# A chunkwise mLSTM cell with a gated MLP: the first chunk's attention in halves of 64 tokens, two batches at a time, and keys and queries loaded ahead of all else

## The chip, the cores and the metric

The kernel runs on one core of a Trainium2 chip. The time is that of one execution on the device in microseconds (us), as a median of several runs. A core has TensorE (PE: matmuls; PEld: its weight loads), VectorE (DVE), ScalarE (ACT), GpSimd (POOL) and SyncE (SP, which issues all the DMAs here). Each engine works through its own instructions in order and waits for the others by semaphores.

## What is computed

The first part is an mLSTM cell, a recurrence over tokens with a matrix state for each of 4x8 heads of width 40:

```python
# B, H, S, D = 4, 8, 768, 40
for t in range(S):
    m_new = np.maximum(f_gate[:, :, t] + m, i_gate[:, :, t])
    f_stab = np.exp(f_gate[:, :, t] + m - m_new)
    i_stab = np.exp(i_gate[:, :, t] - m_new)
    m = m_new
    C = f_stab[:, :, None, None] * C + i_stab[:, :, None, None] * np.einsum('bhd,bhe->bhde', vt, kt)
    n = f_stab[:, :, None] * n + i_stab[:, :, None] * kt
    h_tilde = np.einsum('bhde,bhe->bhd', C, qt)
    denom = np.maximum(np.abs(np.einsum('bhd,bhd->bh', n, qt)[:, :, None]), 1.0)
    y[:, :, t] = 1.0 / (1.0 + np.exp(-o_gate[:, :, t])) * h_tilde / denom
```

Its output, as 3072 tokens of 320 columns, goes through an MLP: `h = x @ w_in` (320 to 2048 columns), `g = h * sigmoid(1.702 h)`, `g @ w_out` (back to 320). The weights come as 64-bit floats, which the kernel turns into 32-bit ones itself.

## The kernel before

The 768 tokens are cut into 6 chunks of L = 128, for all 4 batches at once (512 tokens of the MLP per chunk). Chunk w needs: its gates' running sums (`gates`), the decay factors as columns (`columns`), keys and queries with head width on partitions (`transposes`), weights between tokens (exponentials of gate differences times scores), the sum over values (`values`), the carried state, and the normalised and gated result (`outputs`) transposed for the MLP (`seam`). Then the up-projection runs over 8 pairs of 128 hidden columns (`up` for chunk 0, `up_fast` for the others), then the down-projection in blocks. The attention of chunk w+1 is put between the down blocks of chunk w by a list written out by hand (`attention`).

Chunks from 1 on work in halves of HL = 64 tokens and on two batches at a time (index c): the scores are then 64x64 blocks on the diagonal, the state is carried to the middle of the chunk (`state_mid`) and to its end, and each half gets its share from the state before it. There `slot(i, x)` says in which half of the 128 partitions the half x of the heads of parity i lies; parities 0 and 1 lie crossed, so that the blocks use all four corners of the TensorE array.

Chunk 0 is different before the change. It has no state before it, and its attention is done on whole blocks of 128x128 tokens, one batch b at a time. `weights(0, b)` adds up the exponents on TensorE in PSUM: a mask (L366), then for each head the running maximum `m3` (L370) and the gate sums `a3` (L371), both split in three 16-bit parts, and ACT takes Exp (L373). `scores(0, b)` multiplies queries and keys (L390), and DVE multiplies the two (L392). `values(0, b)` is one matmul per head (L432). One `carry` per two batches gives the state at the chunk's end (L493), copied by ACT (L497), between the up-projections of chunk 0; `scale` (L483, on POOL) weights the values for it.

The order of the start is that of the program text: the loads are issued on SP by `load` (L121, keys, queries, values, gates of one batch) and `fetch` (L166, a piece of the MLP weights); the pieces are turned into 32-bit floats by `convert`, two operations on ACT (L234, L235) and four on DVE (L236 to L241). `up(0, 0)` needs pieces 0 to 2. `keep_busy(n)` puts n matmuls without use on TensorE (L189). The loop at L718 interleaves transposes, scores, weights and two converts; the loop at L731 does values, outputs and seams; L765 starts `up`, whose first matmul is L515. PSUM tiles come from two pools: `banks` gives pairs of banks from `ps_a` (two such tiles), other tiles come from `ps_m` (four, one of which belongs to the idle matmuls).

Of the kernel before, what the change touches and what calls it, by code (L numbers as in the profile page):

```python
# [26 lines left out]
def kernel(  # L27
# [140 lines left out]
    wt = {(0, b): gp.tile([L, NP, 2, L], FP, tag="g", name="wt") for b in range(B)}  # L168
    load_gates(0)
    for b in range(B):  # L170
        load(0, "kq", slice(b, b + 1))
        if b:
            fetch(b - 1)
    for b in range(B):
        load(0, "vo", slice(b, b + 1))
    for n in range(3, 10):
        fetch(n)
# [3 lines left out]
    idle, ident_b, neg_mask = (small[:, n * 128:n * 128 + 128] for n in range(3))  # L181
    pick = small[0:3 * BH, 384:384 + BH]
    a3, m3 = (small[0:3 * BH, n * 128:n * 128 + 128] for n in (4, 5))
    V.memset(idle, 0.0)
    p_idle = ps_m.tile([128, W], FP, tag="m", name="p_idle")

    def keep_busy(n):
        for _ in range(n):
# [13 lines left out]
    G.affine_select(out=neg_mask, in_=neg_mask, compare_op=OP.is_ge, fill=NEG, base=0, pattern=[[1, L]],  # L202
                    channel_multiplier=-1)
# [15 lines left out]
    for t in (k_0, q_st):  # L219
        G.memset(t[:, :, D:DP], 0.0)  # L220
# [23 lines left out]
    def gates(w):  # L244
# [37 lines left out]
        for x, (old, new) in enumerate(((m, mid), (mid, end)) if w else ((m, end),)):  # L282
            t = slice(x * HL, x * HL + HL) if w else slice(0, L)
            V.tensor_scalar(out=st[BH:2 * BH, t], in0=m_run[:, t], scalar1=old, scalar2=None, op0=OP.subtract)
            V.tensor_scalar(out=st[2 * BH:3 * BH, t], in0=a[:, t], scalar1=new, scalar2=-1.0, op0=OP.subtract,
                            op1=OP.mult)
# [4 lines left out]
        if w:  # L291
            dec[w] = gate.tile([BH, 2, BH // 2], FP, name="dec")
            both = gate.tile([BH, 2], FP, name="both")
            V.tensor_tensor(out=both[:, 0:1], in0=m, in1=mid, op=OP.subtract)
            V.tensor_tensor(out=both[:, 1:2], in0=mid, in1=end, op=OP.subtract)
            for x in range(2):
                V.tensor_scalar(out=dec[w][:, x, :], in0=pair, scalar1=both[:, x:x + 1], scalar2=None, op0=OP.mult)

    def slot(i, x):

        return slice((x ^ i) * HL, (x ^ i) * HL + HL)
# [10 lines left out]
    def columns(w):  # L312
        pt = banks("p_cols")[:, 0, :]
        st = stacked[w]
        if w:
            T.matmul(pt[:, 0:3 * BH], st[0], keep, start=True, stop=False)
            T.matmul(pt[:, 0:3 * BH], st[1], swap, start=False, stop=True)
        else:
            T.transpose(pt[:, 0:3 * BH], st, full)
        n = 3 * BH  # L320
        if w in dec:
            n += BH
            T.matmul(pt[:, 3 * BH:n], half.rearrange("p a b -> p (a b)"), dec[w].rearrange("p a b -> p (a b)"),
                     start=True, stop=True)
        c = cols[w] = gate.tile([L, 4 * BH], FP, name="cols")
        V.tensor_copy(out=c[:, 0:BH], in_=pt[:, 0:BH])
        A.activation(out=c[:, BH:3 * BH], in_=pt[:, BH:3 * BH], func=AF.Exp, scale=-1.0)
        if w in dec:
            A.activation(out=c[:, 3 * BH:n], in_=pt[:, 3 * BH:n], func=AF.Exp)
# [4 lines left out]
    def transposes(w, b):  # L334
        for dst, name in ((kT, "kT"), (qT, "qT")):
            dst[w, b] = work.tile([128, NP, L], FP, tag=name, bufs=4, name=name)
        pt = banks("p_t")
        for x, src in enumerate((k_of(w), q_st)):
            for p in range(NP):
                h = b * H + 2 * p  # L340
                T.transpose(pt[:, x, p * L:(p + 1) * L], src[:, h:h + 2, :].rearrange("p a b -> p (a b)"), ident)  # L341
        for x, (dst, copy) in enumerate(((kT, A.copy), (qT, V.tensor_copy if w else A.copy))):
            copy(out=dst[w, b].rearrange("r j t -> r (j t)"), in_=pt[:, x, :])
# [8 lines left out]
    def spread(w):  # L352

        for c in range(2):
            x = wt[w, c] = work.tile([L, NJ, 2, HL], FP, tag="wt", bufs=2, name="wt")
            for i in range(2):
                for n in range(2):
                    src = m_row[w][c * PH + i:(c + 1) * PH:2, n * HL:(n + 1) * HL]
                    nc.sync.dma_start(out=x[slot(i, n), :, i, :], in_=src.unsqueeze(0).to_broadcast([HL, NJ, HL]))

    def weights(w, c):
        if w == 0:
            x = wt[w, c]
            pw = banks("p_w").rearrange("s i (p t) -> s i p t", t=L)
            for i in range(2):
                T.matmul(pw[:, i], ident_b, neg_mask.unsqueeze(1).to_broadcast([L, NP, L]), start=True, stop=False)  # L366
                for p in range(NP):
                    h = c * H + 2 * p + i
                    one = pick[:, h:h + 1].to_broadcast([3 * BH, L])
                    T.matmul(pw[:, i, p, :], one, m3, start=False, stop=False)  # L370
                    T.matmul(pw[:, i, p, :], a3, one, start=False, stop=(p == NP - 1))  # L371
            for i in range(2):
                A.activation(out=x[:, :, i, :], in_=pw[:, i], func=AF.Exp)  # L373
            return
# [9 lines left out]
    def scores(w, c):  # L384
        if w == 0:
            pw = [ps_m.tile([L, NP, L], FP, tag="m", name="p_s") for _ in range(2)]
            for p in range(NP):
                for i in range(2):
                    r = slice(i * 64, i * 64 + D)
                    T.matmul(pw[i][:, p, :], kT[w, c][r, p, :], qT[w, c][r, p, :], start=True, stop=True)  # L390
            for i in range(2):
                V.tensor_tensor(out=wt[w, c][:, :, i, :], in0=pw[i], in1=wt[w, c][:, :, i, :], op=OP.mult)  # L392
            return
        pw = banks("p_s")
        for j in range(NJ):
            b, p = 2 * c + j // NP, j % NP
            for i in range(2):
                r = slice(i * 64, i * 64 + D)
                for x in range(2):
                    t = slice(x * HL, x * HL + HL)  # L400
                    T.matmul(pw[slot(i, x), i, j * HL:(j + 1) * HL], kT[w, b][r, p, slot(i, x) if w == 1 else t],  # L401
                             qT[w, b][r, p, t], start=True, stop=True)
# [22 lines left out]
    def values(w, c):  # L425
        if w == 0:
            hs = slice(c * H, (c + 1) * H)
            po = ps_m.tile([L, H, D1], FP, tag="m", name="p_o")
            for p in range(NP):
                for i in range(2):  # L430
                    h = 2 * p + i
                    T.matmul(po[:, h, :], wt[w, c][:, p, i, :], v_st[:, c * H + h, :], start=True, stop=True)  # L432
            outputs(w, hs, po)
            return
# [3 lines left out]
        for j in range(NJ):  # L438
            for i in range(2):
                for x in range(2):  # L440
                    t, r = slice(x * HL, x * HL + HL), slot(i, x)
# [43 lines left out]
    def carry(w, c):  # L485
        js = slice(c * NJ, (c + 1) * NJ)
        pc = banks("p_c")
        n = 2 if 0 < w < NW - 1 else 1
        for j in range(NJ):
            for i in range(2):  # L490
                for x in range(n):
                    t = slot(i, x) if w else slice(0, L)
                    T.matmul(pc[i * 64:i * 64 + 64, x, j * D1:(j + 1) * D1], k_cols(w, t, c * PH + 2 * j + i),  # L493
                             vw[w, c][t, 2 * j + i, :], start=True, stop=True)
        new = lambda x: pc[:, x, 0:NJ * D1].rearrange("r (j d) -> r j d", d=D1)
        if w == 0:
            A.copy(out=state[1][:, js], in_=new(0))  # L497
            return
        for x, dst in enumerate((state_mid, state[1 - w % 2])[:n]):
            if x:  # L500
                decay(w, c, x, V)
            V.tensor_tensor(out=dst[:, js], in0=new(x), in1=dst[:, js], op=OP.add)
# [209 lines left out]
    gates(0)  # L712
    G.memset(k_1[:, :, D:DP], 0.0)
# [3 lines left out]
    G.memset(v_st[:, :, D:D1], 1.0)  # L717
    for b in range(B + 1):  # L718
        if b < B:
            transposes(0, b)  # L720
        if b:
            scores(0, b - 1)
        if b < B:
            weights(0, b)
        if 0 < b < 3:
            convert(b - 1)
    load(1, "kq")
    load_gates(1)
    columns(0)
    keep_busy(4)  # L730
    for b in range(B + 1):  # L731
        if b < B:
            hs = slice(b * H, (b + 1) * H)
            A.activation(out=eo[0][:, hs, :], in_=eo[0][:, hs, :], func=AF.Tanh, scale=0.5)
            values(0, b)
            if b == 1:
                convert(2)
            keep_busy(2)
        if b == B:
            keep_busy(3)  # L740
        if b:
            seam(0, (b - 1) // 2, ((b - 1) % 2,))
# [12 lines left out]
    def attention(w):  # L755
        at = (0, 1, 3, 4, 8, 9, 10, 11, 13) if w == 1 else (0, 1, 2, 4, 6, 7, 8, 9, 11)
        calls = [[(columns, w), (decay, w, 0, 0), (decay, w, 1, 0), (scale, w, 0), (scale, w, 1)],
                 [(weights, w, 0)], [(weights, w, 1), (open_gates, w)], [(carry, w, 0), (carry, w, 1)],
# [3 lines left out]
    for w in range(NW):  # L762
        more = w + 1 < NW
        if w == 0:
            for j in range(NF // 2):  # L765
# [5 lines left out]
                if j < B:  # L771
                    (carry if j % 2 else scale)(0, j // 2)
# [77 lines left out]
```

## Time and profile before

| what | value |
|---|---|
| median of 3 runs (486.65 to 486.68) | 486.67 us |
| the profiled execution | 486.67 us |
| its span, from first to last instruction | 485.0 us |
| first matmul of the first up-projection (L515) | 34.09 us |
| TensorE busy, 0 to 34.09 | 31.50 us, idle matmuls included |
| DVE, ACT, POOL busy, 0 to 34.09 | 22.98, 16.57, 9.77 us |
| DMA engines busy, 0 to 34.09 | 0.97 of the time, 209 GB/s |
| TensorE busy, 34.09 to 76.14 | 42.05 us of 42.05 |

The profile lists instructions with their engine, the line in the code, the tiles (out<-in) and shapes. A matmul in 32-bit floats appears as two records. The chain of work that ended last is followed back from the last instruction: at each step to what released it, or to the instruction before it on its engine. Times in a timeline are from the start of the span.

### The profile page before, as it was taken

To read this page: it belongs to the slowest core of one execution; us is meant where nothing else is said; L and a number is where in the kernel's file an instruction comes from. 1 tells how busy PE (TensorE), PEld (TensorE's weight loads), DVE (VectorE), ACT (ScalarE), POOL (GpSimd) and SP (SyncE) were. 2 spreads that over 40 slices of the span, in tenths; PEclk is the share of its full clock that TensorE was granted. 3 is DMA by queue.
4 is the path that set the end of the run, shared out by engine and by line. 5 is a ranking of instruction groups with operands and counts; after the bars stand their busy time and mean duration, and the time that the engine had idled before them with its cause. 6 is when DMAs were issued, how large, how long until landed. Compare 5 with 4: busy or idle time off the path is not lost.

```text
span 485.0 us, 12103 instructions
## 1 busy us (share of the span) xinstructions
PE 479.3 (99%) x5016; PEld 388.0 (80%) x5016; DVE 344.0 (71%) x680; ACT 195.3 (40%) x434; POOL 149.7 (31%) x145
## 2 busy tenths in 40 slices
PE   8999999999999999999999999999999999999997
PEld 5774447777767999767999877999876999876997
DVE  6675976988778966768967668968677958343812
ACT  3746557801453901444811354720264630164200
POOL 6020003400398610127620136630035640035300
PEclk9999999999999999999999999999999999999999
DMA  8999995005992000999000899000799000000000
GB/s 176 182 285 146 254 206 153 2 18 103 208 157 45 3 30 3 174 185 139 1 31 3 153 189 158 1 31 3 127 195 165 10 30 3 29 0 1 0 28 27
DMA packets 130790, 44.31 MB, mean 91 GB/s; under 512 B 105616, under 2 KB 128176, under 8 KB 130736
## 3 DMA queue, kind: packets, MB, share of 16 engines
q1 hardware_dynamic: 130736, 43.55, 50.3%
q8 instruction: 39, 0.64, 0.6%
q14 instruction: 15, 0.12, 0.1%
HBM read 39.52 MB, written 4.01 MB: 90 GB/s over the span
## 4 chain that ended last, share of the span: by engine, by line
PE 95%; DVE 3%; POOL 1%; ACT 0%; issue 0%; POOLq 0%; DVEq 0%
PE p_out L687 32%; PE p_h L585 26%; PE p_h L590 8%; PE p_out L636 7%; PE p_h L515 6%; PE p_c L493 3%; PE p_o L442 2%; PE p_s L401 2%; PE p_i L450 2%; PE p_h L521 2%; PE p_x L466 1%; PE p_t L341 1%; PE p_o L432 1%; PE p_s L390 0%; DVE wt L392 0%
## 5 line engine op out<-in xcount | busy, mean ns | idle before, releaser
L627 POOL TENSOR_TENSOR g<-g,parts 128x512 f32<-128x512 f32 x30 | 38.3, 1276 | 124.4 <-DVE parts L619 113.3
L687 PE MATMUL p_out<-w_out_sb,g 128*128 128x160 f32 x480 | 71.0, 302 | 0.0
L687 PEld LDWEIGHTS p_out<-w_out_sb,g 128*128 128x128 f32 x480 | 66.6, 190 | 0.9
L585 PE MATMUL p_h<-xT,w_in_sb 128*128 128x256 f32 x240 | 66.9, 388 | 0.0
L566 ACT ACTIVATE g<-g 128x512 f32<-128x512 f32 x80 | 50.0, 631 | 35.3 <-DVE g L622 24.8
L585 PEld LDWEIGHTS p_h<-xT,w_in_sb 128*128 128x128 f32 x240 | 43.8, 190 | 20.2 <-issue 7.6
L468 ACT COPY xT<-p_x 128x768 f32<-128x768 f32 (+1 forms) x14 | 9.9, 707 | 114.1 <-PE p_x L466 114.1
L692 DVE TENSOR_TENSOR o_sb<-o_sb,p_out 128x160 f32<-128x160 f32 x70 | 21.0, 316 | 44.2 <-PE p_out L687 43.8
L687 PE MATMUL p_out<-t_sb,s 128*128 128x160 f32 x320 | 47.1, 300 | 0.0
L687 PEld LDWEIGHTS p_out<-t_sb,s 128*128 128x128 f32 x320 | 44.4, 190 | 0.2
L618 DVE TENSOR_TENSOR t_x<-p_h,parts 128x256 f32<-128x256 f32 x40 | 16.8, 419 | 38.9 <-PE p_h L590 34.3
L585 PE MATMUL p_h<-t_x,s_in 128*128 128x256 f32 x160 | 41.1, 379 | 0.0
L590 PE MATMUL p_h<-xT,w_in_x 64*128 64x512 f32 x160 | 39.7, 615 | 0.0
L377 ACT ACTIVATE wt<-wt,cols 128x64 f32<-128x64 f32 x160 | 38.8, 338 | 0.0
L423 POOL COPY y<-y 128x128 f32<-128x128 f32 (+1 forms) x14 | 4.0, 285 | 108.7 <-DVE y L420 108.7
L636 PE MATMUL p_out<-w_out_sb,g 128*128 128x320 f32 x128 | 36.3, 437 | 0.0
L585 PEld LDWEIGHTS p_h<-t_x,s_in 128*128 128x128 f32 x160 | 30.4, 190 | 4.1
L615 ACT COPY parts<-p_h 128x256 f32<-128x256 f32 x40 | 14.9, 374 | 45.9 <-PE p_h L585 45.9
L636 PEld LDWEIGHTS p_out<-w_out_sb,g 128*128 128x128 f32 x128 | 23.6, 190 | 9.2 <-DVE w_out_sb L241 0.2
L619 DVE TENSOR_TENSOR parts<-p_h,t_x 128x512 f32<-128x512 f32 x40 | 27.7, 692 | 4.2
L626 ACT COPY g<-p_h 128x512 f32<-128x512 f32 x30 | 17.4, 580 | 30.5 <-PE p_h L590 25.2
L515 PE MATMUL p_h<-xT,w_in_sb 128*128 128x512 f32 x64 | 29.5, 604 | 0.1
(192 smaller groups left out, 897.5 us busy)
## 6 DMA issues: line engine op xcount, KB each, us to landing
wt<-m_row SPq DMA_DIRECT2D x40, 128.0 KB, 4.3
k_sq<-in_k_dram SPq DMA_DIRECT2D x16, 320.0 KB, 5.9
q_sq<-in_q_dram SPq DMA_DIRECT2D x16, 320.0 KB, 10.1
out_dram<-o_sb SPq DMA_DIRECT2D x24, 160.0 KB, 1.8
eo<-in_o_gate_dram SPq DMA_DIRECT2D x5, 640.0 KB, 10.0
bits<-in_moe_w_in_dram SPq DMA_DIRECT2D x6, 512.0 KB, 9.0
v_st<-in_v_dram SPq DMA_DIRECT2D x14, 160.0 KB, 5.2
bits<-in_moe_w_out_dram SPq DMA_DIRECT2D x6, 320.0 KB, 4.8
```

Of the source, the lines that this page charges most:

```text
L377: A.activation(out=x[:, h, :], in_=x[:, h, :], func=AF.Exp, scale=-1.0, bias=cols[w][:, c * PH + h:c * PH + h + 1])
L515: T.matmul(ph[j][i], w_in_sb[:, c, f * 128:(f + 1) * 128], x[:, c, :], start=(first and c == 0), stop=(not first and c == 1))
L566: A.activation(out=gs[w, j][:, i, :], in_=gs[w, j][:, i, :], func=AF.Gelu_apprx_sigmoid)
L585: T.matmul(out, a, x[n], start=start, stop=stop)
L590: T.matmul(row, w_in_x[r, j, :], rest_x[r, 2, :], start=not late, stop=late)
L618: V.tensor_tensor(out=u2, in0=both[:, 1, right], in1=y[:, left], op=OP.add)
L619: V.tensor_tensor(out=y[:, half_w:3 * half_w].rearrange("p (a t) -> p a t", a=2), in0=flat[:, half_w:3 * half_w].rearrange("p (a t) -> p a ...
L626: A.copy(out=g[:, 0, :], in_=row0)
L627: G.tensor_tensor(out=g0, in0=g0, in1=u, op=OP.add)
L636: T.matmul(po, gs[w, f // 2][:, f % 2, b * L:(b + 1) * L], w_out_sb[:, f, :], start=(f == 0), stop=(f == NF - 1))
L687: T.matmul(po, a(f), b[:, f, :], start=(f == 0), stop=(f == NH - 1))
L692: V.tensor_tensor(out=dst, in0=x, in1=po, op=OP.add)
```

## The change

Chunk 0 takes the halves too. `slot` gets the chunk: in chunk 0 half x lies in half x of the partitions, for both parities. `weights`, `scores` and `values` lose their branch for chunk 0; a new function `exponents` adds its exponents on TensorE for two batches, by halves. Chunk 0 now has a `dec` and a middle state, `columns(0)` makes the decay columns for it, `carry` takes the list of halves to do, the first state is set to zero, and the two halves of the carry stand apart: the one to the middle before `values`, the one to the end between the up-projections. Keys and queries of all batches are loaded first; values and output gates are loaded for two batches at a time, between the first two weight pieces. Two pad fills go from POOL to DVE. The order of the start is written anew.

```diff
-    wt = {(0, b): gp.tile([L, NP, 2, L], FP, tag="g", name="wt") for b in range(B)}
+    wt = {}
     load_gates(0)
     for b in range(B):
         load(0, "kq", slice(b, b + 1))
-        if b:
-            fetch(b - 1)
-    for b in range(B):
-        load(0, "vo", slice(b, b + 1))
-    for n in range(3, 10):
+    load(0, "v", slice(0, 2))
+    fetch(0)
+    load(0, "v", slice(2, 4))
+    load(0, "o", slice(0, 2))
+    fetch(1)
+    load(0, "o", slice(2, 4))
+    for n in range(2, 10):
         fetch(n)
...
     V.memset(idle, 0.0)
+    for t in (k_0, q_st):
+        V.memset(t[:, :, D:DP], 0.0)
...
-    for t in (k_0, q_st):
-        G.memset(t[:, :, D:DP], 0.0)
...
-        for x, (old, new) in enumerate(((m, mid), (mid, end)) if w else ((m, end),)):
-            t = slice(x * HL, x * HL + HL) if w else slice(0, L)
+        for x, (old, new) in enumerate(((m, mid), (mid, end))):
+            t = slice(x * HL, x * HL + HL)
...
-    def slot(i, x):
-
-        return slice((x ^ i) * HL, (x ^ i) * HL + HL)
+    def slot(w, i, x):
+
+        n = x ^ i if w else x
+        return slice(n * HL, n * HL + HL)
...
+    def exponents(c):
+
+        x = wt[0, c] = work.tile([L, NJ, 2, HL], FP, tag="wt", bufs=2, name="wt")
+        pw = banks("p_w")
+        for i in range(2):
+            for r in (slice(0, HL), slice(HL, L)):
+                T.matmul(pw[r, i, :], ident_b[:, r], neg_mask.unsqueeze(1).to_broadcast([L, NJ, HL]), start=True,
+                         stop=False)
+            hs = pick[:, c * PH + i:(c + 1) * PH:2].unsqueeze(2).to_broadcast([3 * BH, NJ, HL])
+            for r in (slice(0, HL), slice(HL, L)):
+                T.matmul(pw[r, i, :], a3[:, r], hs, start=False, stop=False)
+            for j in range(NJ):
+                h = c * PH + 2 * j + i
+                for r in (slice(0, HL), slice(HL, L)):
+                    T.matmul(pw[r, i, j * HL:(j + 1) * HL], pick[:, h:h + 1].to_broadcast([3 * BH, HL]), m3[:, r],
+                             start=False, stop=(j == NJ - 1))
+        A.activation(out=x.rearrange("s j i t -> s i j t"), in_=pw.rearrange("s i (j t) -> s i j t", t=HL), func=AF.Exp)
...
-    def carry(w, c):
+    def carry(w, c, xs):
...
+        for x in xs:
+            new, dst = pc[:, x, 0:NJ * D1].rearrange("r (j d) -> r j d", d=D1), (state_mid, state[1 - w % 2])[x]
+            if w == x == 0:
+                A.copy(out=dst[:, js], in_=new)
+                continue
             if x:
                 decay(w, c, x, V)
-            V.tensor_tensor(out=dst[:, js], in0=new(x), in1=dst[:, js], op=OP.add)
+            V.tensor_tensor(out=dst[:, js], in0=new, in1=dst[:, js], op=OP.add)
...
     gates(0)
+    G.memset(v_st[:, :, D:D1], 1.0)
+    G.memset(state[0], 0.0)
...
+    transposes(0, 0)
+    transposes(0, 1)
+    exponents(0)
+    scores(0, 0)
+    transposes(0, 2)
+    exponents(1)
+    convert(0)
+    transposes(0, 3)
+    columns(0)
+    scores(0, 1)
+    for c in range(2):
+        scale(0, c)
+    for c in range(2):
+        carry(0, c, (0,))
     load(1, "kq")
     load_gates(1)
...
+    convert(1)
+    for c in range(2):
+        hs = slice(c * PH, (c + 1) * PH)
+        A.activation(out=eo[0][:, hs, :], in_=eo[0][:, hs, :], func=AF.Tanh, scale=0.5)
+        keep_busy(3)
+        values(0, c)
+    convert(2)
+    keep_busy(6)
+    seam(0, 0)
+    keep_busy(6)
+    seam(0, 1)
     keep_busy(2)
...
-                    (carry if j % 2 else scale)(0, j // 2)
+                    run([(carry, 0, j // 2, (1,)) if j % 2 else (scale, 0, j // 2)])
```

In the changed program the first matmul of the first up-projection is at L504, the values at L433, the state's share at L441, the outputs' first two passes at L447 and L448, the carries at L482, the scores at L401, the scaling at L474.

## The prediction

> **What bounds the kernel now.** I read the page first, then the chain of work that ended last, then the timeline of the first 36 us, and the DMA issues there one at a time.
>
> ```profile
> span 485.0 us, 12103 instructions
> PE 479.3 (99%) x5016; PEld 388.0 (80%) x5016; DVE 344.0 (71%) x680; ACT 195.3 (40%) x434; POOL 149.7 (31%) x145
> ...
> PE 95%; DVE 3%; POOL 1%; ACT 0%; issue 0%; POOLq 0%; DVEq 0%
> ```
>
> TensorE is busy throughout, but what it does early counts: of the start, some matmuls are idle ones. The chain in order of time (start, length, what):
>
> ```profile
> 19.42 0.61 DVE wt L392
> 20.07 1.16 PE p_s L390 x14
> ...
> 21.46 0.87 PE p_idle L189 x4
> ...
> 33.56 0.49 ACT xT L468
> 34.09 3.70 PE p_h L515 x8
> ...
> 43.34 1.06 PE p_c L493 x32
> ...
> 98.84 2.02 PE p_s L401 x128
> ...
> 108.80 0.93 PE p_i L450 x64
> ...
> 389.09 1.99 PE p_c L493 x64
> ```
>
> Until 34.09 us the chain changes engine at nearly every step: the first chunk's attention is a sequence of waits. From 34.09, where the first up-projection starts, it stays on TensorE. By stages, TensorE is busy 42.05 of the 42.05 us from 34.09 to 76.14. So the change is worth the move of one moment, T, the start of the first up-projection (L515 before, L504 after), plus whatever it adds behind T. The work behind T is nearly the same; only T has to be worked out.
>
> **Durations from the trace.** The last chain rows price TensorE's small matmuls. Scores that visit four 64x64 corners of the array take 2.02/128 = 0.016 us a record (L401), the state's share 0.93/64 = 0.0145 (L450). Where only two corners are visited (the last chunk's carry at 389.09) it is 1.99/64 = 0.031; with 128 rows and 64 columns (43.34) 1.06/32 = 0.033. The timeline gives the rest:
>
> ```profile
> 1.06 3.60 PE L189 MATMUL p_idle<-t_sb 128*128 128x512 bf16 x8 [1.06 <-DVE t_sb L184]
> ...
> 33.10 2.53 POOL L483 TENSOR_TENSOR vw<-v_st,cols 128x656 f32<-128x656 f32 x2
> ...
> 34.64 1.28 DVE L236 TENSOR_SCALAR w_in_sb<-w_in_sb 128x512 f32<-128x512 f32 x1 [1.79 <-ACT w_in_sb L234]
> ...
> 105.45 0.84 DVE L456 TENSOR_TENSOR u<-p_i,cols 128x656 f32<-128x656 f32 x1 [0.98 <-PE p_i L450]
> ...
> 108.59 0.90 DVE L420 SCALAR_TENSOR_TENSOR y<-eo,den 128x320 f32<-128x320 f32 x2
> ```
>
> One `outputs` over two batches runs from 105.45 to 109.49: 4.04 us, of which the first two passes (L456, L457) take 1.75. One `scale` on POOL is 1.27. A `convert` is 0.69 from ACT's start to DVE's, then 2.46 on DVE (13.41 to 15.87).
>
> **The change part by part, as a walk to T.**
>
> *Loads.* Before, keys and queries of batches 0 and 1 land at 4.4, 5.5, 6.3 and 7.4 (issue plus time to landing), the first weight piece at 9.3, batch 2 at 10.1 and 10.7, the second piece at 12.5, batch 3 at 13.3 and 14.4. After, all eight come first. The queue is full either way, so each transfer keeps its own service time: batches 2 and 3 took 0.73, 0.62, 0.80 and 1.09 after the landing ahead of each, which brings the last query in at 10.6 instead of 14.4. The price is the first weight piece: the four transfers of values took 0.43, 0.77, 0.97 and 0.94, two of them make 1.6, its own service is 1.9; it lands at 14.2 instead of 9.3. Values and output gates go in four transfers instead of eight, with the same bytes: values complete near 15.8, gates near 21, each before its use below. SP's later items follow the same bytes and do not move: the last two input pieces landed at 37.1 and 38.6, chunk 1's keys behind them.
>
> *DVE ahead of the gates.* Two pad fills move from POOL to DVE. POOL took 0.81 and 0.73; DVE's fill of 64 columns 0.11. Between 0.11 and 0.81 I take 0.6 each (DVE's single-source 128x512 rows of 0.42, scaled to 768). The gate chain, which was just in time for its DMA at 2.6, slips some 0.7, and and with eight small operations for halves (four of 0.24, two of 0.14, two of 0.18, 1.6 in all) in place of two wide ones ends near 9.0. It is hidden: TensorE needs POOL's split exponents (7.03 before, about 7.6 after), and batch 1's queries are transposed only by 8.0. Without cover it would add at most 0.8. POOL's zeroing of the first state (656 columns, about 0.7 by the 0.81 row) ends near 10.5, and POOL has nothing to do before 17.9.
>
> *Exponents per half.* Per call 8 matmuls of 512 columns and 32 of 64 replace, for two batches, 4 of 512 and 32 of 128. If the two column halves run together, as the 0.033 row says, 4x0.22+32x0.016 = 1.4; if nothing runs together, 8x0.22+32x0.055 = 3.5 (0.055 is the spacing of the 128-column rows). I take 1.6, near the first, because the 128x64 row is the same shape. So: exponents 8.0 to 9.6; ACT's one Exp over 1024 columns 1.05 (between 0.80 for 768 and 1.25 for 1280), to 10.75; scores 32x2x0.016 = 1.0; transposes 0.9; second exponents 11.5 to 13.1; Exp to 14.25. The first convert sits behind it on ACT and needs the piece of 14.2: it starts at **14.35**, against 12.72 before. Queued behind it on ACT: batch 3's copies; on DVE: the copy of the decay columns.
>
> *The new detour through the state.* This is what halves add. DVE finishes the convert at 17.5, copies columns (0.18), ACT's Exp (0.22) ends at 17.95; POOL scales twice, 2.53, to 20.5; the second carry runs 20.6 to 21.65 (32 records at 0.031 to 0.033); ACT copies the middle state (0.43) to 22.15; the second convert and the tanh of the gates queue behind that copy on ACT, the first needed at once, the tanh (done 24.7) only at 27.9. Meanwhile TensorE has almost nothing.
>
> *Values and outputs.* Three idle matmuls (0.65), then 64 records of values at 0.031 = 2.0, because row half and column half are now the same half and only two corners are visited; then 64 at 0.0145 = 0.93: ends 25.25. DVE's second convert, released by ACT at 22.15, ends at 25.25 too. First two passes to 27.1, the rest to 29.4. The second values need the PSUM bank that the second pass frees: 27.15 to 30.1. Its outputs: 30.15 to 34.2. POOL's copy of the tail (0.13+0.29) to 34.6, four transposes 0.5, ACT's copy of 768 columns 0.8 with its hand-over: **T = 36.0**, 1.9 later than 34.09. Removed on the way, and of no use since TensorE was waiting: scores fall from 4x1.16 to 2x1.0, DVE's products from 8x0.64 to 2x1.2, exponents from 4x1.34 to 2x1.6.
>
> *Behind T.* The carries between up-projections keep 32 records at about 0.033: nothing. DVE has the third convert later, to about T+3.0 behind POOL's repeated scale (the 1.28 row shows what a scale does to a convert that should take 0.42); the matmul that needs it comes at T+3.63. DVE's four added 0.5 us state operations wait for the carries, so chunk 1's gates end 2.7 later relative to T and the queries' copies about 1.0 later; the 2.10 us that DVE idles before its copy at 76.08 takes that up. Were this cover gone, each uncovered microsecond would go straight onto TensorE.
>
> **A rule weighed.** The first eight idle matmuls take 3.60/8 = 0.45 us each, four later ones 0.87/4 = 0.22: TensorE starts at half speed here. The changed walk leaves it with one 0.5 us burst between 14.9 and 19.3. The Trainium skill, page "TensorE: Matmul & The Clock Gate", Part 1, says that the clock falls to half after an idle window of about 3.4 us. No run here shows such a fall; by the rule, taken strictly, each gap is some 2 us and costs nothing, so the sum stays; if a nearly idle window counts, it becomes the second case below.
>
> **The sum.** 485.0+1.9 = 486.9 of span; the execution profiled took 486.67, 1.67 more than its span and equal to the median. **488.6 us.**
>
> **Rivals.**
> *TensorE slows in the gap.* For it: the 0.45 rows, and 3.9 of 4.4 us without work. Against: the gap is broken by a burst. If the next 4 to 5 us of work run at half speed, less the 0.8 that waits for POOL anyway: second carry +1.05, idle +0.65, part of the values +0.6 gives 2.3: 490.9.
> *The front is later.* Exponents whose halves do not run together end the second Exp 3.8 later (2x1.9), which is 492.4; half way, 490.5. The first weight piece at the slowest pace seen (six steps of 1.1 per 160 KB after 7.4, then 1.9) lands at 15.9 and gives 490.2. Against: each needs its far bound.
> *Not slower.* TensorE runs two-corner streams at the four-corner pace, 0.016 a record: the second carry -0.5, the second values -0.95, the two carries behind T -0.55 each, together -2.55: 486.0. For it: two thirds of the small matmuls run so. Against: the row at 389.09. It ends within 0.2% from 0.025 a record down. That keys come first and nothing follows is no rival: they do, but scores were not what came last.
>
> **Chances.** Forecast 0.47 (own range 487.6 to 489.6: 0.9 less if the bank is free early, as DVE itself is from 29.4, and the front 0.15 sooner; 1.0 more with the fills' 0.8 uncovered and slower hand-overs), slowed TensorE 0.22, late front 0.14, not slower 0.17. By 0.2% (1 us, about what this measurement can tell): faster 0.09, from the third rival with a share of the low front; within 0.14, the rest of it and the forecast's edge; slower 0.77. The range reaches to 486.2 and 491.4.
>
> **What would show it.** Right: L504 starts near 36; POOL's first scale near 18; the second values wait for the pass L448; values at 0.031 a record. Wrong: the first convert starts before 13 or after 16; values at 0.016; idle matmuls of 0.43 after 18 us; TensorE idle between 36 and 78 us.

## The result and the profile after

| | before | after |
|---|---|---|
| median of the runs side by side | 486.66 us (486.63 to 486.68) | 498.25 us (497.88 to 499.05) |
| ratio, 95% interval | | 1.024 (1.022 to 1.026) |
| execution profiled: time, span | 486.67, 485.0 | 499.05, 497.3 |
| first up-projection (T) | 34.09 | 45.40 |
| TensorE clock granted, mean over the span | 1.0 from 5.3 us on | 0.976 |

Slower, as forecast, but by 11.6 us and not 1.9. Of the span's 12.3 us, 11.31 lie ahead of T. In the trace of after the first gelu comes 11.31 us later than in before, the sixteenth 11.30 later, and the last 12.30 later: another 0.99 us is lost far behind T. (The gelu is ScalarE's operation on each block of the up-projection; 96 of them mark the way through a run.)

The chain of waits of after, in order of time (start, length, what):

```profile
8.90 7.17 DMA s_in<-in_moe_w_in_dram
...
16.10 0.66 ACT w_in_sb L238
...
19.37 0.23 ACT cols L328
...
19.73 1.29 POOL vw L474
...
21.07 3.64 PE p_c L482 x64
24.71 1.40 PE p_idle L194 x3
26.11 3.46 PE p_o L433 x61
...
38.06 2.67 PE p_idle L194 x6
40.73 1.28 PE p_x L457 x6
...
44.55 0.81 ACT xT L459
...
45.40 3.70 PE p_h L504 x8
```

The steps are the predicted ones, in the predicted order: weight piece, first convert, columns, scale, carries, values, seams. Until the scale they are 1.8 us late. From 21 us on it is not the waits that are long but the matmuls: three idle ones take 1.40 us (0.65 was priced), 61 records of values 3.46 (0.057 each; priced 0.031), six transposes 1.28.

Busy time of each engine in stretches of after (columns: the stretch and its length; PE, PEld, DVE, ACT and POOL busy with their instructions; granted clock; DMA share; GB/s):

```profile
10.00:15.00 5.00, 5.00 (x131) 4.12 (x127) 1.67 (x5) 3.03 (x4) 0.36 (x1) 1.00 1.25 230
15.00:20.00 5.00, 1.23 (x64) 0.95 (x60) 3.00 (x6) 2.49 (x6) 0.27 (x1) 0.91 0.70 136
20.00:25.00 5.00, 3.93 (x65) 3.62 (x66) 0.47 (x1) 0.67 (x2) 2.27 (x2) 0.50 1.05 239
...
35.00:40.00 5.00, 5.00 (x95) 3.65 (x94) 2.29 (x5) 0.00 (x0) 0.29 (x1) 0.50 1.03 224
40.00:45.00 5.00, 4.94 (x22) 2.98 (x20) 4.69 (x10) 1.25 (x2) 2.69 (x3) 0.70 1.22 146
45.00:50.00 5.00, 4.60 (x14) 1.94 (x16) 4.73 (x8) 3.91 (x6) 0.89 (x1) 1.00 1.03 177
```

After TensorE's poor stretch of 15 to 20 us (1.23 of 5 us busy) the granted clock is 0.50. It stays there although TensorE is busy without a break from 25 to 40 us; the trace's clock record gives a half clock from 19.09 to 42.99, 23.9 us. In before the same stretches look like this, and the clock stays at 1.00 to the span's end:

```profile
15.00:20.00 5.00, 4.48 (x47) 3.46 (x44) 4.65 (x10) 4.01 (x8) 0.00 (x0) 1.00 1.03 151
20.00:25.00 5.00, 4.93 (x44) 4.28 (x45) 2.86 (x9) 2.28 (x6) 0.00 (x0) 1.00 1.13 206
```

### The profile page after: what moved, and what is told of

Same layout as the page of the kernel before. It is cut to its first block, busy times and chain, and to the rows that moved or that the text cites. A ratio compares the mean times of both kernels' runs of the same rounds, so it can differ in the third digit from the quotient of the medians.

```text
span 497.3 us, 12759 instructions
## 1 busy us (share of the span) xinstructions
PE 486.4 (98%) x5349; PEld 392.1 (79%) x5349; DVE 349.1 (70%) x682; ACT 193.1 (39%) x425; POOL 152.2 (31%) x145
## 4 chain that ended last, share of the span: by engine, by line
PE 95%; SPq 2%; DMA 1%; DVE 1%; ACT 0%; issue 0%; POOL 0%; POOLq 0%; DVEq 0%
PE p_out L676 31%; PE p_h L574 25%; PE p_h L579 8%; PE p_out L625 7%; PE p_h L504 6%; PE p_o L433 4%; PE p_c L482 3%; PE p_i L441 3%; PE p_s L401 2%; PE p_x L457 2%; PE p_h L510 2%; PE p_idle L194 1%; DMA s_in<-in_moe_w_in_dram 1%; SPq L121 1%; PE p_t L345 1%; PE p_cols L324 0%
## 5 line engine op out<-in xcount | busy, mean ns | idle before, releaser
L459 ACT COPY xT<-p_x 128x768 f32<-128x768 f32 x12 | 9.6, 799 | 123.5 <-PE p_x L457 123.5
L423 POOL COPY y<-y 128x128 f32<-128x128 f32 x12 | 3.7, 304 | 106.3 <-DVE y L420 106.3
L504 PE MATMUL p_h<-xT,w_in_sb 128*128 128x512 f32 x64 | 29.5, 604 | 0.5 <-ACT xT L459 0.5
L615 ACT COPY g<-p_h 128x512 f32<-128x512 f32 x30 | 17.4, 580 | 30.1 <-PE p_h L579 25.1
## 6 DMA issues: line engine op xcount, KB each, us to landing
v_st<-in_v_dram SPq DMA_DIRECT2D x7, 320.0 KB, 10.6
```

What stands on the lines that cost most here:

```text
L504: T.matmul(ph[j][i], w_in_sb[:, c, f * 128:(f + 1) * 128], x[:, c, :], start=(first and c == 0), stop=(not first and c == 1))
L615: A.copy(out=g[:, 0, :], in_=row0)
```

## The experiments

"T" is the start of the first up-projection; "half clock" is the stretch, in us, in which the clock record of the profiled run gives a granted clock of 0.5; "behind T" is by how much more the last gelu of the run is late against before than the first. The run before of each comparison stood at 486.66 to 486.80 us.

| run | median (range), us | ratio (95%) | T | half clock | behind T |
|---|---|---|---|---|---|
| after | 498.25 (497.88 to 499.05) | 1.024 (1.022 to 1.026) | 45.40 | 19.09 to 42.99 | 0.99 |
| e7 loads alone | 502.43 (502.0 to 502.7) | 1.032 (1.031 to 1.034) | 49.99 | 18.63 to 49.35 | 0.00 |
| e8 attention alone | 503.54 (503.15 to 505.2) | 1.036 (1.034 to 1.038) | 47.63 | 19.40 to 43.29 | 3.01 |
| e2 piece early | 497.75 (496.07 to 500.14) | 1.024 (1.020 to 1.028) | 42.72 | 17.82 to 38.30 | 1.07 |
| e3 columns first | 494.65 (494.01 to 496.05) | 1.017 (1.015 to 1.018) | 41.30 | 18.36 to 38.84 | 2.09 |
| e1 warm gaps | 496.10 (492.94 to 499.12) | 1.019 (1.015 to 1.024) | 42.85 | 34.09 to 40.91 | 0.81 |
| e4 dense after gap | 499.79 (498.89 to 500.33) | 1.027 (1.025 to 1.028) | 43.94 | 18.94 to 29.18 | 2.91 |
| e5 before, no idle matmuls | 490.05 (488.83 to 491.54) | 1.007 (1.004 to 1.010) | 34.46 | 24.30 to 37.95 | 0.08 |
| e6 columns first, warm | 494.61 (491.64 to 495.72) | 1.015 (1.012 to 1.019) | 38.01 | none | 3.00 |
| e9 as e6, 30 cut | 493.22 (492.35 to 496.53) | 1.015 (1.011 to 1.018) | 40.32 | 33.95 to 37.37 | 0.01 |
| e13 after, cut | 498.04 (496.72 to 498.77) | 1.023 (1.021 to 1.025) | 45.76 | 19.37 to 43.27 | 0.19 |
| e10 reordered | 489.68 (488.70 to 490.98) | 1.005 (1.004 to 1.007) | 34.49 | none | 2.96 |
| e11 as e10, cut | 492.98 (492.48 to 493.70) | 1.013 (1.011 to 1.014) | 40.65 | 30.33 to 37.15 | 0.00 |
| e12 as e10, cut, conversion moved | 493.07 (492.58 to 494.18) | 1.013 (1.012 to 1.015) | 40.60 | 26.73 to 36.97 | 0.03 |
| e15 as e10, late cut | 488.33 (487.89 to 490.13) | 1.004 (1.003 to 1.005) | 34.63 | none | 0.00 |
| e14 further reordered | 488.45 (487.32 to 490.25) | 1.004 (1.002 to 1.005) | 35.44 | none | 0.03 |

### Which part costs it: loads or attention

e7 is the kernel before with the new load order, e8 the changed kernel with the old one:

```diff
 # e7, in the kernel before
-    for b in range(B):
-        load(0, "kq", slice(b, b + 1))
-        if b:
-            fetch(b - 1)
+    for b in range(B):
+        load(0, "kq", slice(b, b + 1))
+    load(0, "v", slice(0, 2))
+    fetch(0)
...
```

> The kernel before with the changed kernel's order of loads alone (keys and queries of all batches, then v, first weight piece, v, o, second weight piece, o, the rest). Theory (the load order costs only what the first weight piece is late, and the conversions have room in the kernel before): 486.0 to 488.0, clock 1.0. Rival (the load order carries a good part of the loss, since the first piece lands at 16 us and everything behind it on ScalarE and VectorE shifts): 489 to 492.

> The changed kernel with the order of loads of the kernel before. Theory (the attention in halves with its gap and its 64x64 products makes the loss, by the clock): the clock falls at 18 to 25 us and the time is 495 to 500. Rival (the load order makes it): 487.5 to 490, clock 1.0.

Each alone costs more than both together: +15.8 and +16.9 us against +11.6. Both exceed what I expected, e7 by 10 us and more (both of its ranges were wrong), e8 by 3.5: in e7 the clock stays down longest. In e7 the first weight piece lands at 14.97 instead of 9.3; its convert (ACT, 14.99 to 16.2) stands ahead of batch 3's copies, and TensorE waits 2.10 us for the copy of qT. Two stretches of e7:

```profile
15.00:20.00 5.00, 2.83 (x23) 2.36 (x22) 3.44 (x6) 3.15 (x6) 0.00 (x0) 0.86 0.85 173
...
35.00:40.00 5.00, 5.00 (x24) 4.52 (x24) 3.16 (x9) 0.85 (x2) 0.37 (x1) 0.50 1.09 235
```

The clock falls at 18.63, and 24 matmuls in 5 us, without a gap between them, do not bring it back for 30.7 us. In e8 the values land from 18.8 on, late for the new order of work: TensorE waits 5.3 us for POOL's scale, and the clock falls too (at 19.40). So the parts do not add: the attention in halves needs the new order of loads, its early values above all, and both parts are priced by the clock.

### What makes the clock fall: an idle gap?

Four edits of after, in the order e2, e3, e1, e4:

```diff
 # e2: the first weight piece behind batch 1's keys and queries
         load(0, "kq", slice(b, b + 1))
+        if b == 1:
+            fetch(0)
     load(0, "v", slice(0, 2))
-    fetch(0)
 # e3: the first conversion behind columns, scores, scales
-    convert(0)
     transposes(0, 3)
...
         scale(0, c)
+    convert(0)
 # e1: idle matmuls in both gaps
     columns(0)
+    keep_busy(15)
     scores(0, 1)
+    keep_busy(9)
 # e4: a dense block ahead of the first values
-        keep_busy(3)
+        keep_busy(3 if c else 16)
```

> The changed kernel with the first weight piece loaded behind the keys and queries of batch 1, as before the change. Theory on the front: the convert of that piece then starts when the second Exp ends, near 14.4 instead of 16.1, and all behind it comes 1.7 us earlier. TensorE is then nearly idle for 4.4 us instead of 5.5: if the clock still halves, the time is near 496.5, if it holds, near 488.7. If the first piece was not what ended the wait, the time stays near 498.

> The changed kernel with the first convert moved behind the decay columns, the scores and the scaling in the program's order, so that the columns no longer queue behind a weight piece on ACT and DVE. Theory: POOL's first scaling starts near 15.9 instead of 19.7, its second when the values of batches 2 and 3 have landed (17.3), TensorE has no gap over about 1 us, the clock holds at 1.0, the first up-projection starts near 35.4, time near 488.0. Rival (corner streams alone halve the clock): 0.5 again, time 494 to 496.

> The changed kernel with 15 idle matmuls before the second scores and 9 before the carries, so that TensorE is never idle between 14.9 and 21.1 us; nothing else differs. Theory (the granted clock halves because TensorE is nearly idle from 15.6 to 21.1 us): the clock stays 1.0 from 5 us on, values run at 0.031 a record instead of 0.057, the first up-projection starts near 37.7 instead of 45.4 and the time is near 490.5. Rival (the streams on 64x64 corners load the array so little that the clock halves by themselves): clock 0.5 again from about 20 to 43 us, time near 498. Second rival (the clock matters little, the engines' waits are longer than walked): clock 1.0 but the time above 495.

> The changed kernel with 16 idle matmuls (128x128 by 512 columns) instead of 3 before the first values, so the gap and the fall of the clock stay. Theory (the clock comes back after one window of some 3.4 us of full-array work, which the corner streams do not count as): clock 1.0 again from 28 to 32 us, first up-projection near 44, time near 496.7 although 13 matmuls are added. Rival (the clock stays halved for a fixed time or until the up-projection): the idle matmuls take 0.43 each, all behind comes 5.6 us later, time near 503.5.

e2 and e3 still lose the clock, at 17.82 and 18.36. e2 shortens the waits of TensorE (0.56 and 0.38 us ahead of the fall; one of 2.06 for POOL's scale runs over it), and in e3 no wait of TensorE in that stretch is longer than 0.9 us, against my expectation. e1 holds the clock until 34.09 and loses it in a stall of another kind (below). Up to there it shows what the half clock costs in the unchanged order of work:

```profile
21.39 1.99 PE p_c L482 x64
...
24.13 1.93 PE p_o L433 x61
...
28.10 2.00 PE p_o L433 x61
...
31.46 3.98 issue
```

From the start of the scale to the end of the second values e1 takes 11.8 us (19.30 to 31.1), after 18.3 (19.73 to 38.06), and the same rows of after are 3.64 and 3.46 long. e4 gets the clock back at 29.18, at the end of its dense block, as expected. Its time did not follow: T is 43.94, 1.46 us ahead of after's and as expected, but 2.91 us are lost behind T where after loses 0.99.

e5 asks the opposite of the kernel before, whose 17 idle matmuls between columns and T are taken out:

```diff
-    keep_busy(4)
...
-            keep_busy(2)
-        if b == B:
-            keep_busy(3)
...
-    keep_busy(2)
```

> The kernel before, without the 17 idle matmuls that stand between its columns and its first up-projection. Theory (the granted clock follows how much of the TensorE array is at work in a stretch of some 3.4 us, not whether TensorE is ever idle): in the profiles so far the clock fell at the end of stretches in which the array was used 3, 13, 14 and 26% (time busy x share of rows and columns) and held in stretches of 33% and more. Without the idle matmuls the kernel before comes down to some 20% between 22 and 33 us, so the clock falls at 26 or 33 us and comes back 7 to 14 us later; the up-projection from 34 us runs at half for some of that: 490 to 492 us. Rival (only an idle stretch of 3.4 us or more does it): TensorE is never idle so long there, the clock stays at 1.0, and the time is 486.0 to 486.9.

The clock falls, and comes back at 37.95: the first up-projection starts only 0.37 us later than in before, but its first products run at half, and the first gelu is 2.09 late. The stretch of e3 in which its clock falls:

```profile
15.00:20.00 5.00, 3.53 (x120) 3.14 (x111) 3.68 (x5) 2.28 (x6) 2.58 (x2) 0.84 0.64 121
```

Two stretches of e5:

```profile
20.00:25.00 5.00, 4.89 (x41) 4.89 (x42) 4.29 (x15) 2.76 (x7) 0.24 (x1) 0.93 1.02 179
25.00:30.00 5.00, 5.00 (x26) 5.00 (x25) 3.80 (x10) 0.99 (x3) 0.60 (x2) 0.50 0.97 326
```

In e5 TensorE counts as busy for 4.89 of 5 us and the clock falls in that very stretch. What is low there is not the time but the use: 41 matmuls of 41 columns.

I therefore counted work: columns streamed, at 0.213 us for 512 columns of bf16 and twice that for fp32 (the spacings in these traces), times the share of rows and columns of the array in use, as a share of each 3.41 us (the clock record's stretches are multiples of 3.41). It is an estimate from the shapes and starts of the matmuls. The stretch that ended in a fall had 0.08 (after, e1, e4, e13), 0.16 (e8), 0.21 (e3), 0.22 (e9, e11), 0.25 (e12), 0.27 (e7), 0.30 (e2) and 0.36 (e5). The lowest that held were 0.40 (before), 0.39 (e6), 0.36 (e15), 0.35 (e10), 0.32 (e14) and 0.30 (e1, e11). So use of the array ranks the stretches, though falls and holds overlap between 0.30 and 0.36, and this count gives no sharp boundary. Busy time ranks them worse: e5 fell in a stretch in which TensorE was busy throughout. So do the columns streamed alone, without the share of the array: the stretches of e2 and e3 that ended in a fall have over 1 (products in two corners run side by side), and before held with 0.40. At half clock the corner products reach 0.15 to 0.35, and no stretch under 0.37 was followed by a rise: once down, this attention did not bring the clock back by itself. The Trainium skill, page "TensorE: Matmul & The Clock Gate", Part 1, gives "after ≥1 idle window (~3.4µs)" as the condition for the fall; the windows agree, idleness does not (e5). Its section on psum-queue depth-cycling has a clock that goes up and down because of short pauses between groups of matmuls; e3 has such pauses, e5 has next to none, so they are not what the falls share.

### With the clock held

e6 is e3 with idle matmuls at every wait and, in values, one in every fourth step:

```diff
+    keep_busy(4)
     scores(0, 1)
+    keep_busy(3)
...
+    keep_busy(6)
     for c in range(2):
+        keep_busy(2)
         carry(0, c, (0,))
...
-        keep_busy(3)
+        keep_busy(4)
         values(0, c)
...
+            if w == 0 and j % 4 == 3:
+                keep_busy(1)
```

> As the run with the columns first (first conversion behind columns, second scores and scales), with idle matmuls: 4 before the second scores, 3 behind them, 6 and then 2 and 2 before the carries, 4 instead of 3 before each values, and 1 in every fourth step of the 64x64 products in values. By the theory of array use every stretch of 3.4 us now has 40% or more, the clock stays at 1.0, the first up-projection starts at 36.5 to 38 us and the time is 488.5 to 490.5. Rival one (the 64x64 products alone pull the clock down whatever stands between them): clock down at 18 or 25 us, 493 to 496. Rival two (with the clock held there is still the wait of TensorE for nothing that the profile shows, 3.98 us in the run with warm gaps): clock 1.0 for the most part and 491.5 to 493.

The clock holds and T falls from 45.40 to 38.01, as expected (36.5 to 38). The time does not reach 490.5: 3.0 us are lost behind T. TensorE's waits in e6 show what they are:

```profile
PE p_i L443 <- issue: 1.6, 3, 1.1
...
PE p_idle L194 <- issue: 1.2, 1, 1.2
```

"issue" is time in which an engine waits for nothing the profile shows. Before has none of it. e1 has one of 4.0 us (3.98, in the rows above), in the middle of idle matmuls.

### The stalls put down to issue

I numbered TensorE's records (matmuls, weight loads, sequencer) from the start of the program. In the 17 profiles, all 30 pauses of TensorE of 0.15 us and more ahead of an instruction that waits for no semaphore stand at number 193 or 194 over a multiple of 256, and end 2.3 to 3.1 us after the start of a 16 KB instruction transfer. After has 662 records more than before ahead of T, so block ends fall at other places of the later chunks' corner products, where TensorE runs through a block fastest. The pauses behind T of e6 add up to 1.9 of its 3.0 us; compared record by record with e9 (below), e6 falls back at these places by more than the pause that the profile shows (1.36 us at the one of 1.13) and hardly anywhere else. One such place in e10:

```profile
184.78 0.23 PE L443 MATMUL p_i<-state,qT 40*64 40x41 f32 x1
186.03 0.25 PE L443 MATMUL p_i<-state,qT 40*64 40x41 f32 x1 [1.02 <-issue]
```

To test this, two runs repeat earlier ones (e9 repeats e6, e13 after) with the same streams, but with idle matmuls cut into narrower ones until the count ahead of T is that of before plus three blocks of 256 (to within 2).

```diff
     def keep_busy(n):
         for _ in range(n):
-            T.matmul(p_idle, idle, idle.unsqueeze(1).to_broadcast([128, 4, 128]), start=True, stop=True)
+            ...
+            for x in range(0, 4, m):
+                T.matmul(p_idle[:, x * 128:(x + m) * 128], idle, idle.unsqueeze(1).to_broadcast([128, m, 128]),
+                         start=True, stop=True)
```

> The run with columns first and idle matmuls everywhere, with 30 of its 512-column idle matmuls cut into two of 256: the same streams and the same TensorE time, but 60 more TensorE instructions ahead of the first up-projection. Why: in the profiles so far TensorE's instructions come in blocks of about 256, and behind the first up-projection the kernels with the attention in halves lost 1.0 to 3.0 us in stalls of 0.4 to 1.5 us inside the 64x64 products of later chunks, which the kernel before and the kernel before with the other load order don't show. The kernel before has 557 TensorE records ahead of its first up-projection, the run with idle matmuls everywhere 1265; with 60 more the difference is 768, three blocks, so that the later chunks meet the block ends where the kernel before meets them. Theory (the stalls depend on where the block ends fall): no stall behind the first up-projection, shift against the kernel before constant to 0.2 us, time 490.0 to 491.0 with a spread of under 0.5 us. Rival (they are a matter of the transfers beside, or of chance): 491.5 to 495.7 as without the cut.

> The changed kernel as it is, but with idle matmuls cut (the first 8 and four in front of the seams into four, the others into two; the same streams), so that the TensorE instructions ahead of the first up-projection are those of the kernel before plus three blocks of 256, less 2. Theory: the clock falls at 18 to 20 us as in the changed kernel, the first up-projection is at 44 to 47 us, and the shift against the kernel before stays constant behind it (in the changed kernel it grows by 0.99 us): 496 to 498.3. Rival: the shift still grows by 0.5 to 3 us behind it.

Behind T, e9 loses 0.01 us where e6 lost 3.00, e13 0.19 where after lost 0.99; e11, e12, e14 and e15, cut alike, lose 0.03 or less. So these stalls belong to places. But a place moved out of the later chunks can land in the front: e9 stalls 1.8 us at record 1217, in the second values, the use of the array drops, and the clock falls; hence its 493.2 instead of the 490 to 491 that I expected. In e13 the clock costs what it cost in after, so after's loss is hardly touched: 498.04, as expected.

### Another order of the first chunk

e10 reorders after: columns behind the first scores, both scales ahead of the second scores, the first conversion behind them, then carry and values batch pair by batch pair:

```diff
+    columns(0)
     transposes(0, 2)
...
     for c in range(2):
         scale(0, c)
+    scores(0, 1)
+    convert(0)
+    keep_busy(1)
     for c in range(2):
+        carry(0, c, (0,))
...
+        keep_busy(2)
+        values(0, c)
+        keep_busy(1)
...
     convert(1)
...
     convert(2)
```

e11 and e12 cut its idle matmuls (e12 also converts the second piece between the two outputs), e15 cuts only those behind the second values. e14 further loads v ahead, the second piece ahead of the gates, and the first carry ahead of the second scores.

> The changed kernel with its first chunk in another order: columns directly behind the first scores, both scales before the second scores, the first conversion behind them, then carry, values for the first two batches, carry, values for the last two, then conversions two and three, then the seams; idle matmuls between (in all 29 behind the first 8). Theory (clock held by array use of 40% and more in every 3.4 us; each product of values waits only for the carry of its own two batches, so VectorE's outputs start at 20 to 21 us instead of 31 us): clock 1.0 throughout, first up-projection at 31 to 33 us, time 483.5 to 486.5 with stalls in the later chunks of 0 to 3 us in that. Rival (weights land too late, or the conversions behind the outputs hold the first up-projections up): first up-projection at 33 to 35 us, or its second half waits; 486.5 to 489. Rival (clock falls): 494 or more.

> As the reordered run, with idle matmuls behind the first 8 cut into two or four so that the TensorE instructions ahead of the first up-projection are those of the kernel before plus three blocks of 256, less 2. Theory (stalls depend on where the block ends fall): no stall in the later chunks, 0.5 to 3 us below the reordered run. Rival: the same as the reordered run.

> The reordered run with the second conversion between the two batches' outputs, and with 25 idle matmuls that run while TensorE would wait (the first 8, and 17 of those behind the second values) cut into two or four, so that the TensorE instructions ahead of the first up-projection are those of the kernel before plus three blocks of 256, plus 1. Theory: clock 1.0 throughout; first up-projection at 34.3 to 35.2 us; no wait of it for the conversion (0.9 us in the reordered run); no stall in the later chunks (3.0 us there); time 486.7 to 488.0. Rival (the stalls come back elsewhere, or the clock falls once): 488.5 to 492.

> The reordered run with the same streams, but with 16 of the last idle matmuls (those between the second values and the first up-projection) cut in two or four: 88 TensorE instructions more, all behind the second values, so that the total ahead of the first up-projection is that of the kernel before plus three blocks of 256, plus 1. In the traces so far every stall put down to issue of more than 0.6 us ended at TensorE record 191 to 194 over a multiple of 256, counted from the start of the program, 2.3 to 2.9 us after the start of a 16 KB instruction transfer. Theory: the front keeps the places of the reordered run (no stall there, clock 1.0, first up-projection at 34.3 to 34.8 us), the later chunks get the places of the kernel before (no stall; 3.0 us in the reordered run); the wait of 0.9 us for the second conversion stays: 487.3 to 488.3. Rival (stalls appear by chance): 488.7 to 491.

> The run with the late cut, and besides: v of the first two batches loaded behind the keys and queries of batch 1, the second weight piece ahead of the output gates, the carry of the first two batches ahead of the second scores (0.44 us of waiting goes), both conversions behind the second scores, one idle matmul less. Theory: first up-projection at 33.2 to 34.0 us, no wait for a conversion, no stall in the later chunks, clock 1.0: 485.8 to 486.8. Rival (array use falls under 37% in the last half of a 6.8 us window and the clock with it, or an issue stall in the front, whose places have moved by a few records): 489 to 493.

e10 brings T to 34.49 with the clock at 1.0, later than the 31 to 33 that I expected; 0.88 us go to waits for conversions and 2.96 to stalls. e11 and e12 remove those stalls and get others in the front (2.6 and 1.7 us, at records 1218 and 961), and with them the clock falls: 3.3 and 3.4 us worse, against my expectation. e15 leaves the front alone but for a stall of 0.29 us, loses nothing behind T and ends at 488.33, at the edge of what was expected (487.3 to 488.3). TensorE in e15:

```profile
27.86 0.23 PE L450 MATMUL p_i<-state_mid,qT 40*64 40x41 f32 x1
28.02 1.70 PE L200 MATMUL p_idle<-t_sb 128*128 128x512 bf16 x15
...
30.67 2.41 PE L200 MATMUL p_idle<-t_sb 128*128 128x128 bf16 x40 [0.29 <-issue]
...
34.63 3.87 PE L513 MATMUL p_h<-xT,w_in_sb 128*128 128x512 f32 x8 [0.44 <-ACT xT L468]
38.88 1.99 PE L519 MATMUL p_h<-xT,w_in_x 64*128 64x512 f32 x8 [0.38 <-DVE w_in_x L252]
```

Values end at 28.0 (38.06 in after) and T is 34.63. Against before the execution profiled loses 0.54 us at T and 0.62 in the first up-projections, which wait for conversions (0.38 of it as the wait shown), together 1.16; its span is 1.2 longer (486.2 against 485.0). Nothing is left over. e14 has no such wait, but its early second conversion keeps DVE from the outputs until 23.66, and T is 35.44 instead of the 33.2 to 34.0 that I expected. No version beat the kernel before.

## Why the prediction was wrong

- **The step that failed is the term for a slowed clock.** The sum put it at nothing ("each gap is some 2 us and costs nothing, so the sum stays"). The rival that had it, ranked second at 0.22, had the mechanism right but only the price of "the next 4 to 5 us of work", 2.3 us; the clock stayed down for 23.9 us. T came 9.4 us after the forecast 36.0. The walk's steps put 1.8 of that ahead of the scale (19.73 against 17.95); the other 7.6 is work from 21 us on at half speed, net of the bank (below). e1 shows it with the order of work unchanged: from the scale to the end of the second values the walk has 12.15 us (17.95 to 30.1), e1 with the clock held 11.8, after 18.3. I let the clock recover as soon as TensorE had work again, and never asked how much of the array that work uses. e5 and e7 show matmuls without a break that do not hold or raise it. e6 and e15, with the clock held, put T at 38.01 and 34.63.
- **The rule weighed was read too strictly.** I took gaps of some 2 us as free because each is shorter than 3.4 us. In after they are 2.8 and 2.1 us and the clock falls; in e3 they are under 1 us, and it falls too.
- **The first weight piece was mis-sized.** Forecast 14.2, landed 16.08: the last query came at 11.37 instead of 10.6, behind it came 1.92 us for the values of two batches (1.6 priced) and 2.79 for the piece (1.9 priced). The convert started at 16.10 instead of 14.35, beyond the bound that I had named as the sign of a wrong walk. The "later front" rival had 15.9 and was rated 0.14. It is worth the 1.8 us above. The later items of SP did not stay where they were either: the last input piece landed at 39.93 instead of 38.57; in after TensorE did not wait for it.
- **Behind T, priced at nothing, 0.99 us were lost.** The cover named (DVE, POOL) held, and TensorE waits for no engine there. What I did not count was instructions: 662 more records shift the block ends. e13 returns 0.8 of it.
- **The bank wait was wrong, in our favour.** "The second values need the PSUM bank that the second pass frees": in e1 they start at 28.10, right behind L447 (27.21 to 28.08) and ahead of the second pass; 0.9 us too much in the walk.
- **Right:** the moment T decides; exponents 1.4 us a call (1.6 taken), Exp 1.03; the corner products at 0.031 to 0.035 a record when the clock is full (32 in 1.13 us in e6 and e10), so "not slower" is out; the fills on DVE hidden; values waiting for the detour through the state. Two of the stated signs of a wrong forecast came: the convert after 16, idle matmuls of 0.47 us after 18.

The chance for slower (0.77) pointed the right way; the range ended at 491.4, since the slowed clock was carried only to 490.9. A rival whose end no row of the trace bounds ought to be carried to the next event that can end it, here the first dense work: the idle matmuls in front of the seams, from 38 us on.

## What to carry to other kernels

Splitting products into corners of the array makes them cheap and leaves the array mostly unused (0.15 to 0.35 in the count above); if such work fills several microseconds, look at its streamed work per 3.4 us, not at TensorE's busy time, and put dense work between, as e1, e6, e10 and e15 do. When a load is moved ahead, follow what stands behind the piece that comes later on each in-order engine: here one late convert on ACT (16.10 us) held up TensorE for 2.8 us, and the low clock that followed everything until the up-projections. Adding hundreds of tiny matmuls also moves the places where instruction blocks end; a change in a far-off stage of about a microsecond with no releaser is a sign of it.

## What was not expected of the hardware

- The granted clock falls while TensorE counts as busy 4.89 of 5 us (e5), and stays at half through 30.7 us of matmuls (e7).
- TensorE stalls of 0.16 to 3.98 us at record 193 or 194 over a multiple of 256 in all 30 cases. The Trainium skill, page "Runtime: NRT & Kernel Launch", section "Instruction fetch mechanics", has blocks of 256 instructions, as the places confirm, and calls crossing one "mostly hidden"; here it is not always, where weight load and matmul pairs of 0.031 us follow each other. Why one stall is 0.2 us and another 3.98 stays open: the two longest in the front (3.98 and 2.59) stood beside busy DMA engines (share 1.04 and 0.98 in the 3 us before), those of up to 1.13 behind T beside idle ones (0.02 to 0.03), but e15's of 0.29 had 0.97 as well; no run took the transfers away.
- The same kernel scatters by up to 6.2 us (e1: 492.94 to 499.12), where before scatters by 0.4 (486.68 to 487.06 over 13 runs): the mean clock of e1's runs goes from 1.0 to 0.986 with it.
